# Gated product before the last bank, moved queue steps and ScalarE copies in long units of a gated attention and feed-forward kernel

## Chip, core and metric

The kernel runs on one core of a Trainium2 chip. The metric is the device time in microseconds of one execution. The engines are TensorE (PE), VectorE (DVE), ScalarE (ACT), GpSimd (POOL) and SyncE (SP), which issues all the transfers.

## The reference

The input is 2048 tokens of 576 features. Two branches are mixed by a gate per token.

```python
g = sigmoid((x * gate_w).sum(-1))
# a: 32 heads of 18, four segments of 512 tokens
for s in range(4):
    p = softmax(q_s @ k_s.T * scale + mask)  # keys later than the query are masked
    a_dot = p @ v_s
    a_mem = (phi(q_s) @ M) / (phi(q_s) @ z + 1e-6)
    o_s = sigmoid(beta) * a_mem + (1 - sigmoid(beta)) * a_dot
    M += phi(k_s).T @ v_s;  z += phi(k_s).sum()
a = concat(o_s) @ wo
# b: hidden size 4608
b = (silu(x @ w_gate) * (x @ w_up)) @ w_down
out = g * a + (1 - g) * b
```

Here phi(t) is t + 1 for positive t and exp(t) otherwise.

## The kernel before

Numbers are kept as pairs: a 16-bit high half and a low half that holds the rounding rest, so that a product is three matmuls. A high half is made by a copy, mostly on ScalarE, and its low half by a subtraction on VectorE or GpSimd.

The first stage runs over the four segments. For each of nine chains `n` (pairs `(m, u)` of a weight tile and q or k) `qk` makes 14 matmuls and casts the result; `mid` is a list of other small work that is put in between. For segments 1 to 3 the generator `upd_gen` adds the memory matrix of the segment before: it transposes phi of the keys and copies it to `kt` (512 columns on ScalarE, L514, and 64 on VectorE, L517). Eight value steps `v_step` and memory reads `mem_step` follow. `RSTEP` places the splits of the last 64 rows of x for the first token half in segment 2: `rest_split(j)` makes one of seven pieces, `rest_sum(j)` one of the sums that some pieces need. `FSUM` and `FSPLIT` place the same for the other rows in segment 3; `first_split(6, ...)` stands behind the first two value steps.

The second stage is the feed-forward part, in two token halves of 1024. Each half has 36 units `f`, one for each 128 hidden columns. A unit computes gate and up products of two token blocks by a scheme of seven products instead of eight, `seven(bank, j)`, j = 0 to 6, seven matmuls each. Block 0's gated row is `sg0`, block 1's `sg1`; `p5` is the up part of block 1. `sg1` needs products 4 and 5, but not product 6; `sg0` needs product 6. `split_by` makes their halves `hh` and `hl` by deferred steps.

Behind each product stands `tick()`, eight steps a unit (0 to 7); step 6 stands right behind step 5, and product 6 between steps 6 and 7. A step first runs what `defer(k, fn)` put off for it: k = 1 is the next step. Then it runs down groups and attention steps. A unit with `q = f % 3 == 0` and f > 0 is a long unit: it carries the 16 down groups of the three units before it (`feed`: eight 128-token tiles `i`, two column halves `hf`), nine matmuls each into one of two banks. Tiles 0 to 3 belong to block 0, tiles 4 to 7 to block 1. `down_end` (L1171, or L1169 for the first three units) adds the bank to `ya` on VectorE and so frees the bank. The groups begin in step 2: 2, 2, 3, 3, 3 and 3 in steps 2 to 7. Behind the last unit of the first half ten steps without products run the remaining 16 groups (`BREAK`).

Attention of all segments runs as a generator, `att_gen`, one bank of a head pair a step `tau`. In a long unit it advances 12 times. In an ordinary pair of heads ScalarE makes the exponential `pe` (L1006), GpSimd clears its upper triangle, then `p1` is its fp16 copy (L1102 on VectorE, L1104 on ScalarE) and `p2` the rest, on GpSimd (L1106). In the second half every second pair is "turned": the maximum is taken first, the exponential is L943, and `c_bank` copies it to fp16 on VectorE (L947) and takes the rest on GpSimd (L948). `later[0]` is true in the second half from unit 1 on.

Down weights are split by `d_split(f)`: ScalarE copy L1139 in the same step, VectorE low half L1140 one step later, a scaled third L1142 or L1144 after that, then a store `dc` for the second half. `rest_second` makes the rest pieces of the second half's tokens in steps behind unit 35. ScalarE's functions Exp and Silu need different tables; `exp_table()` runs a dummy Exp so that the load comes at a chosen place, and `gates()` makes the token gates with Exp.

Each engine runs its instructions in the order in which this program emits them. Units are told below by half and number; "unit 9" is the tenth of the first half.

Of the kernel before, what the change touches and what calls it, by code (L numbers as in the profile page):

```python
# [69 lines left out]
def gated_mix(ctx, tc, xT, xrest, wf, wfr, wfh, wd, wv, wo, beta, cmask, ident, bmask, out):  # L70
# [323 lines left out]
    with ExitStack() as st:  # L394
# [101 lines left out]
        def upd_gen(s):  # L496
            acc = [pair_tile([P, 3, MW]), pair_tile([P, 2, MW])]
            Mo, Mn = Mm[s % 2], Mm[(s + 1) % 2]
            for i in range(5):
# [8 lines left out]
                if i < 4:  # L508
# [8 lines left out]
                    nc.vector.tensor_copy(kt[:, 512:576], tb[:, 64:128])  # L517
# [143 lines left out]
        RSTEP = {2: (0, 3), 3: (5, -1), 4: (1, -4), 5: (4, -2), 6: (2,), 7: (-6,), 8: (6,)}  # L661
# [59 lines left out]
        def scan_load(t):  # L721
# [3 lines left out]
            if t in (21, 30):  # L725
# [3 lines left out]
        FSUM = {3: [(1, 0), (4, 0)], 4: [(2, 0), (1, 1)], 6: [(4, 1), (2, 1)], 7: [(6, 0)], 8: [(6, 1)]}  # L729
        FSPLIT = {2: [(0, 0)], 3: [(5, 0), (0, 1)], 4: [(1, 0), (4, 0)], 5: [(5, 1), (2, 0)], 6: [(1, 1), (3, 0)],  # L730
                  7: [(3, 1), (4, 1)], 8: [(2, 1)]}
        for s in range(NSEG):
            upd = upd_gen(s - 1) if s else None
            casts = []
            for n, (m, u) in enumerate(chains):
# [41 lines left out]
                qk(s, m, u, mid)  # L777
                flush(2)
# [19 lines left out]
            for n in range(8):  # L798
# [44 lines left out]
    with ExitStack() as st:  # L843
# [207 lines left out]
        def att_gen():  # L1051
            N = 10 * NB
            for tau in range(N + TL + VL + 5):
# [236 lines left out]
        later = [False]  # L1290
        turn_of = [()]
# [33 lines left out]
        def feed(half, f):  # L1325
            return [(f // CH, i, hf, hs, ds, half) for i in range(8) for hf in range(2)]
# [43 lines left out]
        def rest_second(rest):  # L1370
# [19 lines left out]
            def low(j):  # L1390
# [3 lines left out]
            todo = [(-1, load, 0), (0, high, 0), (0, high, 3), (1, low, 0), (1, low, 3), (4, load, 1), (11, high, 5),  # L1394
                    (11, total, 1), (12, low, 5), (12, high, 1), (13, total, 4), (13, low, 1), (14, total, 2),
                    (14, high, 4), (15, low, 4), (15, total, 6), (16, high, 2), (16, low, 2), (17, high, 6), (18, low, 6)]
# [37 lines left out]
        for pos, (half, f) in enumerate(seq):  # L1434
# [49 lines left out]
            def tick():  # L1484
# [5 lines left out]
                if half == 0:  # L1490
# [19 lines left out]
            later[0] = half == 1 and f > 0  # L1510
            turn_of[0] = () if pos < 24 else (1, 3)
# [154 lines left out]
```

## Time and profile before

| | |
|---|---|
| three runs | 1718.13, 1721.46, 1721.53 us |
| median | 1721.46 us |
| profiled execution, its own time | 1718.78 us |
| its span | 1717.1 us |
| busy: TensorE, VectorE, ScalarE, GpSimd | 98%, 79%, 63%, 52% |
| granted TensorE clock, mean | 0.998 |

The profile is of one execution. Rows of the order in time give start, duration, engine, line, operation, written and read tiles, shape and count; square brackets give how long the engine was idle before and what ended it. Line numbers are those of the kernel before.

### The profile page before, as it was taken

Reading aid. Unit: us, or ns where it says so; the run is one execution under the profiler, and the core shown is the slowest. Engines: PE = TensorE matmul, PEld = TensorE weight load, DVE = VectorE, ACT = ScalarE, POOL = GpSimd, SP = SyncE. Lnnn points to the kernel's source line nnn. Section 1 sums busy time; section 2 is a strip of 40 time slices with the busy share of each in tenths; the row PEclk is TensorE's granted clock in tenths of the full one; section 3 lists DMA queues with packets and bytes.
Section 4 is the critical chain, followed back from the end, with each engine's and each line's share of the span. In section 5 each row is a group of like instructions: output and inputs, shape, how many; then the busy total and the mean of one; then the engine's idle time right before and its main releaser. Section 6 shows DMA issues by size and latency. Waiting matters only on the chain.

```text
span 1717.1 us, 35318 instructions
## 1 busy us (share of the span) xinstructions
PE 1679.5 (98%) x12269; PEld 1077.8 (63%) x12269; DVE 1353.8 (79%) x3295; ACT 1076.6 (63%) x1930; POOL 889.2 (52%) x1191
## 2 busy tenths in 40 slices
PE   9999999999999999999999999999999999999999
PEld 7898865556655665565555656556656656655577
DVE  6687676789888988898886878788878788776466
ACT  7666567777777777767774654665556566565411
POOL 3336562266667665665452665465546565554121
PEclk9999999999999999999999999999999999999999
DMA  8666675666776675446535486796696597574544
GB/s 282 218 232 222 214 260 208 208 200 177 231 223 208 168 244 192 154 121 195 169 123 164 114 192 158 163 219 136 147 215 166 121 221 167 140 163 125 156 157 145
DMA packets 349542, 314.25 MB, mean 183 GB/s; under 512 B 201268, under 2 KB 266548, under 8 KB 349364
## 3 DMA queue, kind: packets, MB, share of 16 engines
q1 hardware_dynamic: 349364, 312.00, 63.5%
q8 instruction: 96, 1.57, 0.4%
q14 instruction: 82, 0.67, 0.1%
HBM read 186.15 MB, written 99.55 MB: 166 GB/s over the span
## 4 chain that ended last, share of the span: by engine, by line
PE 73%; DVE 12%; ACT 7%; issue 3%; DMA 3%; POOL 1%; SPq 1%; DVEq 0%; ACTq 0%; POOLq 0%
PE bank L1426 31%; PE bank L1162 18%; PE bank L223 8%; PE bank L1429 5%; PE bank L889 3%; PE bank L1002 2%; DVE ya L1171 1%; PE bank L1030 1%; ACT L1540 1%; DVE junk L907 1%; PE bank L1032 1%; PE bank L964 1%; DVE p L1102 1%; ACT row L1540 1%; DMA rc<-rt 1%
## 5 line engine op out<-in xcount | busy, mean ns | idle before, releaser
L1162 PE MATMUL bank<-dw,hh 128*128 128x320 f16 (+1 forms) x2304 | 437.5, 286 | 13.3 <-DVE ya L1171 8.9
L1162 PE MATMUL bank<-dw,hl 128*128 128x320 f16 (+1 forms) x1152 | 330.1, 287 | 3.8 <-DVE hl L1298 3.2
L1106 POOL TENSOR_TENSOR p<-pe,p 128x512 f16<-128x512 f32 x220 | 271.9, 1236 | 75.3 <-DVE p L1102 50.6
L1162 PEld LDWEIGHTS <-hh 128*128 128x128 f16 x2304 | 225.3, 98 | 99.9 <-issue 18.1
L1006 ACT ACTIVATE pe<-bank 128x512 f32<-128x512 f32 x220 | 130.1, 592 | 183.6 <-PE bank L1002 167.5
L1171 DVE SCALAR_TENSOR_TENSOR ya<-bank,sc,ya 128x320 f32<-128x320 f32 x352 | 176.2, 511 | 55.0 <-PE bank L1162 53.3
L1429 PE MATMUL bank<-xr,rh 128*128 128x512 f16 x504 | 191.0, 379 | 0.0
L907 DVE CUSTOM_DVE_ANT_0 junk<-bank,cm 128x128 bf16<-128x128 f32 (+2 forms) x352 | 169.3, 481 | 13.7 <-PE bank L889 7.3
L1298 DVE SCALAR_TENSOR_TENSOR hl<-hh,row 128x512 f16<-128x512 f16 x144 | 129.7, 902 | 45.7 <-ACT hh L1295 44.8
L1014 POOL TENSOR_SCALAR_AFFINE_SELECT pe<-pe 128x256 f32<-128x256 f32 (+1 forms) x220 | 89.3, 406 | 144.9 <-ACT pe L1006 137.3
L1162 PEld LDWEIGHTS <-hl 128*128 128x128 f16 x1152 | 112.7, 98 | 34.3 <-DVE hl L1298 3.8
L889 PE MATMUL bank<-kst,qst 108*128 108x512 bf16 (+3 forms) x512 | 124.5, 299 | 3.6 <-ACT pe L1006 2.9
L1002 PE MATMUL bank<-qst,kst 111*128 111x512 bf16 (+3 forms) x352 | 103.2, 300 | 1.1 <-DVE acc L975 1.1
L1102 DVE CAST p<-pe 128x512 f16<-128x512 f32 x203 | 103.3, 510 | 0.0
L369 POOL TENSOR_TENSOR ws<-raw 128x256 f32<-128x256 f32 x72 | 65.6, 912 | 63.4 <-DMA raw<-in_wf_dram 32.2
L1538 DVE TENSOR_TENSOR row<-bank,row 128x512 f32<-128x512 f32 x72 | 49.6, 689 | 60.9 <-ACT bank L1537 60.8
L223 PE MATMUL bank<-xo,qhi 128*128 128x512 f32 x288 | 92.5, 401 | 1.3 <-ACT xo L132 0.7
L466 POOL TENSOR_TENSOR q<-qr,q 128x512 bf16<-128x512 f32 x36 | 47.8, 1329 | 84.8 <-ACT q L465 77.0
L1295 ACT ACTIVATE hh<-row 128x512 f16<-128x512 f32 x144 | 89.0, 618 | 3.7 <-DVE row L1548 3.0
L1533 ACT ACTIVATE row<-bank 128x512 f32<-128x512 f32 x72 | 42.9, 596 | 73.7 <-PE bank L1429 73.7
L1537 ACT ACTIVATE bank<-bank 128x512 f32<-128x512 f32 x72 | 41.9, 581 | 72.8 <-PE bank L1429 70.9
L1429 PEld LDWEIGHTS <-rh 128*128 128x128 f16 x504 | 49.3, 98 | 59.6 <-issue 0.2
(1102 smaller groups left out, 4213.9 us busy)
## 6 DMA issues: line engine op xcount, KB each, us to landing
xo<-in_wf_dram SPq DMA_DIRECT2D x65, 320.0 KB
raw<-in_wf_dram SPq DMA_DIRECT2D x72, 256.0 KB
dc<-dw SPq DMA_DIRECT2D x36, 432.0 KB
dw<-dc SPq DMA_DIRECT2D x36, 432.0 KB
rh<-rc SPq DMA_DIRECT2D x72, 168.0 KB
draw<-in_wd_dram SPq DMA_DIRECT2D x36, 288.0 KB
xo<-in_xT_dram SPq DMA_DIRECT2D x33, 256.0 KB
vd<-vps SPq DMA_DIRECT2D x8, 912.0 KB
```

The costliest lines, as they stand in the source:

```text
L223: nc.tensor.matmul(t, st[n], mv[n], start=(n == 0), stop=(n == 13))
L889: nc.tensor.matmul(t[:, c:c + w], qs[:KR, pr, P * i:P * i + P], ks[:KR, pr, 0:w], start=True, stop=True)
L907: nc.vector.tensor_tensor_reduce(junk.bitcast(BF)[:, :w], t[:, c:c + w], cm[:, L - w:L], 1.0, -3.0e38, OP.add, OP.max, m[:, k:k + 1])
L1002: nc.tensor.matmul(t[:, c:c + w], ks[:KR + 3, pr, P * j:P * j + P], qs[:KR + 3, pr, P * j:L], start=True, stop=True)
L1006: nc.scalar.activation(pe, t, AF.Exp, scale=SCALE)
L1102: nc.vector.tensor_copy(p1, pe)
L1106: nc.gpsimd.tensor_sub(p2, pe, p1)
L1162: nc.tensor.matmul(t, p, d[:, q, cs], start=(f == CH * c and n == 0), stop=(f == CH * c + CH - 1 and n == 2))
L1171: nc.vector.scalar_tensor_tensor(ya[:, i, cs], t, inv[c], ya[:, i, cs], op0=OP.mult, op1=OP.add)
L1298: nc.vector.scalar_tensor_tensor(lo, hi, -STEP, src, op0=OP.mult, op1=OP.add)
L1426: nc.tensor.matmul(t, w[:, p, z], x[z][:, q], start=first and n == 0, stop=False, skip_group_check=True)
L1429: nc.tensor.matmul(t, rem[:, RPOS[j]], XR[j], start=False, stop=True, skip_group_check=True)
```

## The change

It has these parts.

- The 64-column copy to `kt` is made by ScalarE.
- Segment 2: the sum for rest piece 6 moves from chain 7 to chain 6, and its split from within chain 8 to behind it.
- Segment 3: the sum and split of pieces (6, 1) and (2, 1) move from chain 8 to behind the first value step; both splits of piece 6 follow one value step later.
- The dummy Exp: gone in unit 0 of the first half; in unit 3 the one behind product 0 is gone, and the gates are made behind both Silu rows.
- `sg1`'s product (L1549) comes before product 6: ahead of step 6 in units with q = 0 (all but the very first unit), behind step 6 in the others. Block 1's halves are made first, and the down groups start with tiles 4 to 7.
- Unit 35: the down weights' split is issued in step 2 instead of 5. The rest pieces of the second half from the tenth entry on come two steps later.
- A flag `calm`, true in the long units of the second half: there ScalarE makes `p1` and `c_bank`'s copy.

```diff
-                    nc.vector.tensor_copy(kt[:, 512:576], tb[:, 64:128])
+                    nc.scalar.activation(kt[:, 512:576], tb[:, 64:128], AF.Copy)
...
-        RSTEP = {2: (0, 3), 3: (5, -1), 4: (1, -4), 5: (4, -2), 6: (2,), 7: (-6,), 8: (6,)}
+        RSTEP = {2: (0, 3), 3: (5, -1), 4: (1, -4), 5: (4, -2), 6: (2, -6)}
...
-        FSUM = {3: [(1, 0), (4, 0)], 4: [(2, 0), (1, 1)], 6: [(4, 1), (2, 1)], 7: [(6, 0)], 8: [(6, 1)]}
+        FSUM = {3: [(1, 0), (4, 0)], 4: [(2, 0), (1, 1)], 6: [(4, 1), (2, 1)], 7: [(6, 0)]}
-                  7: [(3, 1), (4, 1)], 8: [(2, 1)]}
+                  7: [(3, 1), (4, 1)]}
...
                 qk(s, m, u, mid)
+                if (s, n) == (2, 8):
+                    rest_split(6)
...
-                    if n < 2:
-                        first_split(6, n)
+                    if n == 0:
+                        first_split(2, 1)
+                        first_sum(6, 1)
+                    if 1 <= n < 3:
+                        first_split(6, n - 1)
...
-            nc.vector.tensor_copy(pq[:, 0:L], lg)
+            if calm[0]:
+                nc.scalar.activation(pq[:, 0:L], lg, AF.Copy)
+            else:
+                nc.vector.tensor_copy(pq[:, 0:L], lg)
...
-                    if later[0] or z % 5 not in turn_of[0]:
+                    if not calm[0] and (later[0] or z % 5 not in turn_of[0]):
...
-            return [(f // CH, i, hf, hs, ds, half) for i in range(8) for hf in range(2)]
+            return [(f // CH, i, hf, hs, ds, half) for i in (4, 5, 6, 7, 0, 1, 2, 3) for hf in range(2)]
...
-            todo = [..., (4, load, 1), (11, high, 5), (11, total, 1), (12, low, 5), ..., (17, high, 6), (18, low, 6)]
+            todo = [..., (4, load, 1), (13, high, 5), (13, total, 1), (14, low, 5), ..., (19, high, 6), (20, low, 6)]
...
-                    if f == 2 and k > 4 or f > 2 and (q, k) in ((1, 1), (1, 7), (2, 5 + int(f < FT - 1))):
-                        g = k - 5 if f == 2 else f - 1 if k == 1 else f
+                    if f == 2 and k > 4 or f > 2 and (q, k) in ((1, 1), (1, 7), (2, 6 if f < FT - 1 else 2)):
+                        g = k - 5 if f == 2 else f - 1 if (q, k) == (1, 1) else f
...
+            calm[0] = half == 1 and q == 0 and f > 0
...
-            if half == 0 and q == 0 and f:
+            if half == 0 and q == 0 and f > CH:
                 exp_table()
-                if f == CH:
-                    gates()
...
             nc.scalar.activation(sg1, y, AF.Silu, scale=iw[f // 4])
-            if (half or q == 0) and not cps:
+            if (half or q == 0 and f) and not cps:
                 exp_table()
+                if half == 0 and f == CH:
+                    gates()
             tick()
+            if q == 0 and pos:
+                nc.vector.scalar_tensor_tensor(sg1, p5, hk[f // 4], sg1, op0=OP.mult, op1=OP.mult)
             tick()
+            if q or not pos:
+                nc.vector.scalar_tensor_tensor(sg1, p5, hk[f // 4], sg1, op0=OP.mult, op1=OP.mult)
             seven(xx, 6, False)
             nc.vector.scalar_tensor_tensor(sg0, xx, hk[f // 4], sg0, op0=OP.mult, op1=OP.mult)
-            nc.vector.scalar_tensor_tensor(sg1, p5, hk[f // 4], sg1, op0=OP.mult, op1=OP.mult)
-            split_by(2, hh[:, 0], hl[:, 0], sg0, int(q < CH - 1))
-            split_by(3, hh[:, 1], hl[:, 1], sg1)
+            split_by(2, hh[:, 1], hl[:, 1], sg1, int(q < CH - 1))
+            split_by(3, hh[:, 0], hl[:, 0], sg0)
             tick()
```

More of the change, by code (lines that the diff above doesn't have):

```diff
@@ L1290, in gated_mix @@
         later = [False]
+        calm = [False]
         turn_of = [()]
@@ L1392, in low @@
                 nc.vector.scalar_tensor_tensor(t, source(j)[32:64], sx[32:64], t, op0=OP.mult, op1=OP.subtract)
-            todo = [(-1, load, 0), (0, high, 0), (0, high, 3), (1, low, 0), (1, low, 3), (4, load, 1), (11, high, 5),
-                    (11, total, 1), (12, low, 5), (12, high, 1), (13, total, 4), (13, low, 1), (14, total, 2),
-                    (14, high, 4), (15, low, 4), (15, total, 6), (16, high, 2), (16, low, 2), (17, high, 6), (18, low, 6)]
+            todo = [(-1, load, 0), (0, high, 0), (0, high, 3), (1, low, 0), (1, low, 3), (4, load, 1), (13, high, 5),
+                    (13, total, 1), (14, low, 5), (14, high, 1), (15, total, 4), (15, low, 1), (16, total, 2),
+                    (16, high, 4), (17, low, 4), (17, total, 6), (18, high, 2), (18, low, 2), (19, high, 6), (20, low, 6)]
             return [(o, lambda fn=fn, j=j: fn(j)) for o, fn, j in todo]
```

## The prediction

> **What bounds the kernel now.** The profile's first part comes first: who is busy.
>
> ```profile
> PE 1679.5 (98%) x12269; PEld 1077.8 (63%) x12269; DVE 1353.8 (79%) x3295; ACT 1076.6 (63%) x1930; POOL 889.2 (52%) x1191
> ```
>
> TensorE is busy 1679.5 of 1717.1 us, so 37.6 us is the most that removing waits can give, apart from stretches where its clock is halved. No matmul is added or removed; the question is which waits go and which come. Hence the view of waits with TensorE as the waiting engine, first for 300 to 900 us (first half), then 940 to 1620 us (second half); columns: total, times, longest.
>
> ```profile
> PE bank L1162 <- DVE ya L1171: 4.8, 8, 1.0
> PE bank L889 <- ACT pe L1006: 2.3, 6, 0.4
> ```
>
> ```profile
> PE bank L1162 <- DVE ya L1171: 4.1, 10, 0.9
> PE bank L889 <- ACT pe L1006: 0.6, 2, 0.3
> ```
>
> In both halves the main wait is for VectorE's accumulation `ya`, which frees a bank of the down product; in the long units VectorE paces the end. Then the busy time by stretches, for the granted clock (the column after POOL) around the two worst places.
>
> ```profile
> 270.00:276.00 6.00, 3.99 (x20) 1.67 (x18) 3.22 (x6) 5.97 (x12) 0.00 (x0) 1.00 0.88 279
> 276.00:282.00 6.00, 5.41 (x26) 3.04 (x26) 3.54 (x10) 2.83 (x8) 1.45 (x2) 0.72 1.01 383
> 901.00:904.00 3.00, 0.54 (x3) 0.21 (x4) 3.00 (x4) 2.35 (x5) 2.00 (x2) 1.00 0.00 0
> 904.00:910.00 6.00, 6.00 (x36) 4.22 (x36) 3.40 (x7) 0.46 (x1) 0.32 (x1) 0.72 0.98 317
> ```
>
> Behind each idle cluster (2.0 of 6 us and 2.5 of 3 us) the mean clock of the next six microseconds falls to 0.72: 0.28 times 6, so 1.7 us of work is lost in each spell, by this estimate.
>
> The Trainium skill, "TensorE: Matmul & The Clock Gate", Part 1, names an idle window of about 3.4 us as what halves the clock, and asks for no idle gap above that. The rows show halving after clusters without so long a gap, so the measurement decides; by the Trainium skill's gap rule no spell would be there to save and the gain below would be 3.4 us smaller.
>
> **The change, part by part.**
>
> *The kt cast to ScalarE* (12 times, segments 1 to 3). Two waits go:
>
> ```profile
> 65.76 0.35 PE L505 MATMUL bank<-vf,kt 128*64 128x76 f32 x2 [1.06 <-DVE kt L517]
> 196.41 0.35 PE L505 MATMUL bank<-vf,kt 128*64 128x76 f32 x2 [0.72 <-DVE kt L517]
> ```
>
> The cast queues on ScalarE right behind the 512-column cast that the same group of matmuls needs anyway, so it is there before its use. ScalarE gets 12 short casts; what stands behind each is the next chain's copy, with three banks in rotation as cover; without it each would cost its own length. Bounds 0 and -1.8; I take -1.8.
>
> *Segment 2: the rest piece 6 moves.* Its subtraction goes to GpSimd one chain earlier, its split behind chain 8.
>
> ```profile
> 158.30 0.74 DVE L249 SCALAR_TENSOR_TENSOR xr<-xo,sc,xr 32x512 f16<-32x512 f32 x1
> 159.07 0.69 DVE L468 SCALAR_TENSOR_TENSOR ph<-bank,ph 128x512 f32<-128x512 f32 x1
> 159.82 0.93 PE L550 MATMUL bank<-Mm,ph 128*128 128x152 f32 x6 [1.35 <-DVE ph L468]
> ```
>
> `ph` no longer stands behind 0.74 us of split. -0.74 is one bound, -1.35 the other, if the earlier subtraction also unblocks VectorE; I take -1.2. Late next is the first value step's own chain.
>
> *Segment 3: pieces (6,1) and (2,1) move behind the first value step.*
>
> ```profile
> 219.96 0.46 DVE L486 TENSOR_TENSOR r<-bank,vps 128x288 f32<-128x288 f32 x1 [0.21 <-ACT vps L485]
> 220.47 1.85 PE L223 MATMUL bank<-vw,xo 128*128 128x288 f32 x12 [0.83 <-DVE r L486]
> ```
>
> VectorE itself waited 0.21 for ScalarE here, so taking a split off VectorE does not bring L486 forward. Bounds -0.83 and +0.75 (one split more, later); I take 0.
>
> *Fewer table loads.* Without the dummy exponential in units 0 and at the head of 3, two Exp loads and the two Silu loads that followed them go.
>
> ```profile
> 245.88 1.28 ACT L1419 ACT_TABLE_LOAD   x1
> 248.53 1.46 PE L1426 MATMUL bank<-xo,wo__2849 128*128 128x512 f16 x6 [0.53 <-ACT bank L1519]
> ```
>
> The load stands ahead of the bank copy that TensorE waits for: -0.5. In unit 3:
>
> ```profile
> 271.50 1.28 ACT L1419 ACT_TABLE_LOAD   x1
> 275.57 0.74 DVE L377 SCALAR_TENSOR_TENSOR wo__3111<-ws,sc,wo__3111 128x512 f16<-128x512 f32 x1
> 275.70 0.30 PE L1162 MATMUL bank<-dw,hh 128*128 128x320 f16 x1 [1.14 <-DVE dw L1140]
> 276.59 0.30 PE L1162 MATMUL bank<-dw,hl 128*128 128x320 f16 x1 [0.59 <-DVE dw L1142]
> 276.72 0.38 PE L1162 MATMUL bank<-dw,hh 128*128 128x256 f16 x2
> ```
>
> ScalarE's `hh`, and behind it VectorE's `hl`, `dw` and the scaled third, come at least 1.28 us earlier. The 1.14 goes; the third still has L377's 0.74 ahead of it, so I leave 0.5 of the second wait: -1.2. With so little idle time left the half-clock spell goes: -1.7. Bounds 0 and -3.4.
>
> *Last unit of the first half.* The down weights' split is issued three steps earlier, the other columns' rest pieces two steps later (five ScalarE copies, five VectorE low halves, four GpSimd subtractions), and the product that needs no last bank is made first and used first.
>
> ```profile
> 900.59 1.36 DVE L1549 SCALAR_TENSOR_TENSOR row<-row,sc 128x512 f32<-128x512 f32 x1
> 901.39 0.45 PE L1162 MATMUL bank<-dw,hh 128*128 128x320 f16 x2 [0.89 <-ACT hh L1295]
> 901.88 1.37 DVE L1142 TENSOR_SCALAR dw<-dw 128x576 f16<-128x576 f16 x1
> 903.90 0.31 PE L1162 MATMUL bank<-dw,hl 128*128 128x320 f16 x1 [2.06 <-DVE hl L1298]
> ```
>
> Of the 2.95 us, the 1.37 leaves the path, and one product of 1.36 runs under the last bank's matmuls: -2.7, and the second spell -1.7. Bounds 0 and -4.7. The rest pieces, two steps later, end inside the next unit, behind its first three products, each issued ahead of its own bank's use; one piece late would cost up to a low half of this shape, 0.74 (L249 above). I take 0. One `dc` store moves forward with the split on the DMA queue; it lands in memory that is read only in the second half.
>
> *The last unit of all*, the same order:
>
> ```profile
> 1632.87 2.42 DVE L1298 SCALAR_TENSOR_TENSOR hl<-hh,row 128x512 f16<-128x512 f16 x2
> 1634.70 0.31 PE L1162 MATMUL bank<-dw,hl 128*128 128x320 f16 x1 [1.10 <-DVE hl L1298]
> ```
>
> The wait ends inside the 2.42 us of the two low halves; no row tells how much of that is their own work and how much is blocking, so an earlier start may not be wholly an earlier end. Bounds 0 and -1.1; -0.5.
>
> *Long units of both halves: the product moved ahead of step 6.* This one costs. In unit 9:
>
> ```profile
> 408.50 0.75 DVE L377 SCALAR_TENSOR_TENSOR wo__4684<-ws,sc,wo__4684 128x512 f16<-128x512 f32 x1
> 409.16 0.55 DVE L1171 SCALAR_TENSOR_TENSOR ya<-bank,sc,ya 128x320 f32<-128x320 f32 x1
> 409.76 0.43 PE L1162 MATMUL bank<-dw,hh 128*128 128x320 f16 x2
> 414.02 0.78 DVE L1549 SCALAR_TENSOR_TENSOR row<-row,sc 128x512 f32<-128x512 f32 x1
> ```
>
> The product now at 414.02 goes in ahead of L377 at 408.50. `ya` ends at 409.71 and the matmul that needs its bank starts at 409.76: no slack. An operation of this kind holds the queue 0.66 (408.50 to 409.16) to 0.78 us, so TensorE waits some 0.7 us more. At the old place it held up nothing: that step shows no wait. Eleven long units of the first half: +7.7. Bounds 0 and +15 (1.36 each, from 900.59). In the short units the product now waits for ScalarE's Silu instead of the last bank; only the other product stands behind it, which waits for that bank anyway: 0.
>
> *Second half, long units: some 130 casts from VectorE to ScalarE* (12 attention steps a unit, one cast each). The busy time of their two lines in the eleven units, then one cast on ScalarE, and from the order in time two rows of unit 15:
>
> ```profile
> sum 388.00, DVE 36.16; mean DVE 3.29
> sum 388.00, DVE 30.76; mean DVE 2.80
> L1104 ACT ACTIVATE p<-pe 128x512 f16<-128x512 f32 x17 | 10.6, 622 | 0.0
> 1242.84 1.28 DVE L1549 SCALAR_TENSOR_TENSOR row<-row,sc 128x512 f32<-128x512 f32 x1
> 1244.57 0.38 PE L1162 MATMUL bank<-dw,hh 128*128 128x256 f16 x2 [0.87 <-DVE ya L1171]
> ```
>
> VectorE gets back 6.1 us in each long unit, more than the 0.7 that the moved product puts before step 6; behind bank 6 the product is gone as well, which is the wait at 1244.57. Up to the whole 4.1 goes. ScalarE takes some 12 times 0.62, 7.3 us a unit. Its own busy time in these units and in the first half's eleven:
>
> ```profile
> sum 388.00, PE 380.19 PEld 258.96 DVE 307.97 ACT 191.75 POOL 204.71; mean PE 34.56 PEld 23.54 DVE 28.00 ACT 17.43 POOL 18.61
> sum 396.70, PE 384.50 PEld 257.94 DVE 339.34 ACT 273.45 POOL 234.38; mean PE 34.95 PEld 23.45 DVE 30.85 ACT 24.86 POOL 21.31
> ```
>
> 17.4 becomes 24.7, as much as the first half bears with its 2.3 us of waits for `pe`, 1.7 more than the second half has now. The casts read what was ready two steps before, so I take a third of that, +0.6, and -4.1 for VectorE: -3.5. Queued behind the casts are the exponentials of the next step and, through `p1`, GpSimd's low halves. Bounds -4.1 and +14 (below).
>
> *Groups in the order 4 to 7, 0 to 3*: as many matmuls, only a match to the order of `hh`: 0.
>
> **The sum.** The idle column starts at a matmul's modelled end: the one at 276.59 lasts 0.30, but the next starts 0.13 later. Each wait removed gives 0.17 more than it shows; some twelve go: -2.0. -1.8 -1.2 -0.5 -2.9 -4.4 -0.5 +7.7 -3.5 -2.0 = -9.1 us. The profiled execution took 1718.78 us (span 1717.1), so 1709.7. It lies at the lower end of the three runs (median 1721.46, lowest 1718.13); I add 1.3, half of that distance: **1711**.
>
> **The rivals.**
> *The moved product is free in the first half.* If VectorE had time in hand before step 6, 7.7 us fall away: 1703. For it: VectorE is 30.85 busy of 36 us. Against it: unit 9's `ya` without slack.
> *The moved product costs 1.3.* It has two inputs in SBUF, and 900.59 and 1242.84 show it at 1.36 and 1.28, against 0.78 at 414.02. At 1.3 in all eleven, 6.6 us more: 1717.6, no change to be measured. The Trainium skill, "SBUF — State Buffer", "SBUF: two separate sides", says that a VectorE operation with two SBUF inputs and a GpSimd operation that reads SBUF block each other for a whole instruction; the spread of the three durations fits it, but the row of a long unit is the short one.
> *The change does not do what it says at units 3 and 35.* Waits remain, and the clock still halves: both spells (3.4) and two thirds of the 3.9 us of waits come back, 6.0: 1717. Against it: both clusters hang on instructions that really move.
> *Slower: ScalarE becomes the bound in the second half's long units.* It has two table loads, 1.28 us each, in step 5, and one cast more for each of 12 steps. If at two steps of each unit a cast of 0.62 lies ahead of an exponential that TensorE waits for, 11 times 1.24 is +13.6, and the 3.5 is not gained: 1728. It decides once more than 9 us of this reach TensorE. Against it: the first half bears the same load.
>
> **How the numbers follow.** Forecast 0.50 (its own range 1704 to 1716); free product 0.20; dear product 0.10; units 3 and 35 unchanged 0.07; ScalarE bound 0.13. Range 1701 to 1722: it leaves out the slower case and the far end of the free one. A measurement of this kernel can tell 0.2%, 3.4 us: faster 0.70, same 0.17, slower 0.13.
>
> **What would show it.** four table loads fewer; no wait for `kt`; the clock at 1.00 behind both places; the wait for `ya` L1171 up from 4.8 to some 12 us in the first half and below 1 in the second; waits for `pe` up slightly. If the first half's `ya` waits stay at 4.8, or the second half's `pe` waits pass 5 us, the prediction is wrong there.

## The result and the profile after

| | before | after |
|---|---|---|
| median | 1719.80 us | 1735.16 us |
| lowest to highest | 1717.06 to 1721.53 | 1734.84 to 1736.13 |
| profiled execution, its span | 1717.1 | 1733.1 |

The ratio is 1.0092, with a 95% interval from 1.0074 to 1.0109: 15.4 us slower, where 9 us faster was forecast. Both medians are over four runs, those of before with one more than were shown. The first part of the page after the change:

```profile
PE 1682.2 (97%) x12269; PEld 1077.7 (62%) x12269; DVE 1315.2 (76%) x3155; ACT 1139.6 (66%) x2064; POOL 878.2 (51%) x1191
```

VectorE is busy 38.6 us less than before and ScalarE 63.0 more, as planned, and yet the kernel is slower. So the loss isn't in a sum of work; it is in where the work stands. The waits of TensorE show where, first for 300 to 900 us (first half), then for 940 to 1640 us (second half). Columns: total, times, longest.

```profile
PE bank L1170 <- DVE ya L1179: 19.7, 13, 2.4
PE bank L894 <- ACT pe L1014: 2.4, 6, 0.4
```

```profile
PE bank L1170 <- DVE ya L1179: 3.7, 5, 1.4
PE bank L894 <- ACT pe L1014: 2.4, 5, 1.0
```

L1170, L1179, L894 and L1014 are L1162, L1171, L889 and L1006 of before. In the first half the wait for `ya` rose from 4.8 to 19.7 us, by 14.9; the span grew by 16.0. (The two aren't parts of one sum. From first matmul to first matmul the ten long units 6 to 33 of the first half grew by 19.7 us in all, and the rest of the kernel got 3.7 shorter.) It isn't more waits so much as longer ones: 2.4 us at the longest, where 1.0 was. In the second half it hardly fell (4.1 to 3.7), and the wait for exponentials rose (0.6 to 2.4). The order in time of unit 9 shows one of the long waits whole; first VectorE, then GpSimd, then TensorE:

```profile
409.13 0.75 DVE L1557 SCALAR_TENSOR_TENSOR row<-row,sc 128x512 f32<-128x512 f32 x1
409.79 1.65 DVE L377 SCALAR_TENSOR_TENSOR wo__4682<-ws,sc,wo__4682 128x512 f16<-128x512 f32 x1
411.36 0.54 DVE L1179 SCALAR_TENSOR_TENSOR ya<-bank,sc,ya 128x320 f32<-128x320 f32 x1
```

```profile
409.36 1.52 POOL L1114 TENSOR_TENSOR p<-pe,p 128x512 f16<-128x512 f32 x1 [1.34 <-PE bank L1010]
```

```profile
411.95 0.43 PE L1170 MATMUL bank<-dw,hh 128*128 128x320 f16 x2 [1.60 <-DVE ya L1179]
```

The product stands ahead of L377 as forecast and holds the queue 0.66 us. But L377, 0.75 us long at this place before, now takes 1.65. The row of GpSimd in unit 9 of the kernel before:

```profile
408.73 1.53 POOL L1106 TENSOR_TENSOR p<-pe,p 128x512 f16<-128x512 f32 x1 [1.34 <-PE bank L1002]
```

There L377, begun at 408.50, was 0.23 us ahead of this subtraction (L1114 after); now the product begins ahead of the subtraction, and L377 comes while the subtraction is under way. 0.66 and 0.90 make 1.56, and TensorE waits 1.60. Some of the waits are followed by a lower clock. Two stretches of the busy time, in units 27 and 30, each with a wait of 1.96 us (the column behind POOL is the granted clock):

```profile
760.00:780.00 20.00, 17.76 (x143) 11.35 (x142) 16.34 (x44) 7.44 (x13) 13.94 (x21) 0.91 0.26 78
820.00:840.00 20.00, 17.54 (x146) 11.66 (x144) 16.74 (x45) 7.60 (x13) 13.88 (x20) 0.91 0.29 82
```

0.09 of 20 us are 1.8 us of work lost in each, by this estimate; these two units grew by 2.8 and 3.1 us, the other long ones of the first half from 6 on by 1.2 to 2.0. The length of a wait alone doesn't decide it: behind the longest one, 2.39 us in unit 6, the clock stays at 1.00.

### The profile page after: what moved, and what is told of

The parts are those of the page before. It is cut to its first block, busy times and chain, and to the rows that moved or that the text cites. A ratio compares the mean times of both kernels' runs of the same rounds, so it can differ in the third digit from the quotient of the medians.

```text
span 1733.1 us, 35354 instructions
## 1 busy us (share of the span) xinstructions
PE 1682.2 (97%) x12269; PEld 1077.7 (62%) x12269; DVE 1315.2 (76%) x3155; ACT 1139.6 (66%) x2064; POOL 878.2 (51%) x1191
## 3 DMA queue, kind: packets, MB, share of 16 engines
q8 instruction: 96, 1.57, 0.4%
## 4 chain that ended last, share of the span: by engine, by line
PE 75%; DVE 9%; ACT 9%; issue 3%; DMA 2%; POOL 1%; SPq 1%; DVEq 0%; ACTq 0%; POOLq 0%
PE bank L1435 30%; PE bank L1170 19%; PE bank L223 10%; PE bank L1438 5%; PE bank L894 3%; PE bank L1010 2%; ACT L1548 1%; PE bank L1038 1%; ACT L1428 1%; ACT row L1548 1%; DVE ya L1179 1%; DVE junk L912 1%; ACT pe L1014 1%; PE bank L505 1%; PE bank L972 1%
## 5 line engine op out<-in xcount | busy, mean ns | idle before, releaser
L1170 PE MATMUL bank<-dw,hh 128*128 128x320 f16 (+1 forms) x2304 | 436.5, 286 | 27.0 <-DVE ya L1179 23.4
L1170 PE MATMUL bank<-dw,hl 128*128 128x320 f16 (+1 forms) x1152 | 330.0, 286 | 0.9 <-DVE dw L1150 0.6
L1114 POOL TENSOR_TENSOR p<-pe,p 128x512 f16<-128x512 f32 x220 | 271.1, 1233 | 65.0 <-DVE p L1110 35.2
L1170 PEld LDWEIGHTS <-hh 128*128 128x128 f16 x2304 | 225.2, 98 | 112.8 <-issue 32.6
L1014 ACT ACTIVATE pe<-bank 128x512 f32<-128x512 f32 x220 | 130.2, 592 | 181.0 <-PE bank L1010 169.8
L1179 DVE SCALAR_TENSOR_TENSOR ya<-bank,sc,ya 128x320 f32<-128x320 f32 x352 | 178.1, 512 | 82.5 <-PE bank L1170 80.7
L1170 PEld LDWEIGHTS <-hl 128*128 128x128 f16 x1152 | 112.5, 98 | 31.9 <-DVE hl L1307 2.9
L894 PE MATMUL bank<-kst,qst 108*128 108x512 bf16 (+3 forms) x512 | 125.0, 299 | 5.5 <-ACT pe L1014 4.8
L1529 ACT ACTIVATE bank<-bank 128x512 f32<-128x512 f32 x72 | 41.9, 582 | 69.5 <-PE bank L1438 59.1
L1545 ACT ACTIVATE bank<-bank 128x512 f32<-128x512 f32 x72 | 41.9, 581 | 65.3 <-PE bank L1438 63.4
```

Of the source, the lines that this page charges most:

```text
L894: nc.tensor.matmul(t[:, c:c + w], qs[:KR, pr, P * i:P * i + P], ks[:KR, pr, 0:w], start=True, stop=True)
L1014: nc.scalar.activation(pe, t, AF.Exp, scale=SCALE)
L1114: nc.gpsimd.tensor_sub(p2, pe, p1)
L1170: nc.tensor.matmul(t, p, d[:, q, cs], start=(f == CH * c and n == 0), stop=(f == CH * c + CH - 1 and n == 2))
L1179: nc.vector.scalar_tensor_tensor(ya[:, i, cs], t, inv[c], ya[:, i, cs], op0=OP.mult, op1=OP.add)
```

## The experiments

In the expectations unit 0.9 is unit 9 of the first half and 1.9 that of the second. A ratio is to the kernel before, measured on the same chip in the same experiment, and a difference to the kernel before is between these two medians. Kernels of different experiments are best compared by their ratios.

**Where the loss is: the product, in the first half.** The changed kernel, with the product ahead in the second half alone:

```diff
-            if q == 0 and pos:
+            if q == 0 and half:
...
-            if q or not pos:
+            if q or not half:
```

> The changed kernel, but in the long units of the first half sg1's product is made behind step 6 again; ahead of it only in the second half. Theory A (the product ahead of step 6 displaces VectorE's other work there, above all the weight split of L377, into GpSimd's subtraction of L1114, and costs 1.5 to 2.1 us in each of the ten long units 6 to 33 and more where the clock falls): the 19.7 us by which these units grew go, and the time is 1735 - 20 = 1715 (1711 to 1719). Theory B (the moved product is nearly free, and the loss of the first half comes with other parts, the new order of groups or the moved splits): 1731 to 1736. Theory C (the moved product costs its 0.66 to 0.7 us of queue and no more, the rest comes with other parts): 1735 - 11 x 0.7 = 1727.

Measured: 1720.9 us, ratio 1.0013 [1.0004, 1.0023], by the two ratios (1.0092 to 1.0013) some 14 us less than the changed kernel. Theory A; but 5.9 us more than it said, so something else costs too. The other way round, this part alone in the kernel before:

```diff
             tick()
+            ahead = half == 0 and q == 0 and f > 0
+            if ahead:
+                nc.vector.scalar_tensor_tensor(sg1, p5, hk[f // 4], sg1, op0=OP.mult, op1=OP.mult)
             tick()
...
-            nc.vector.scalar_tensor_tensor(sg1, p5, hk[f // 4], sg1, op0=OP.mult, op1=OP.mult)
+            if not ahead:
+                nc.vector.scalar_tensor_tensor(sg1, p5, hk[f // 4], sg1, op0=OP.mult, op1=OP.mult)
```

> The kernel before with one edit: sg1's product ahead of step 6 in the long units of the first half. Theory A (product ahead costs 1.5 to 2.1 us in each long unit): 1720 + 11 x 1.8 = 1740 (1736 to 1744). Theory B (product nearly free): 1719 to 1722. Theory C (0.7 us each): 1727.

Measured: 1736.7 us, ratio 1.0110 [1.0096, 1.0124], +17.8 us from one instruction moved in eleven units. Its waits from 300 to 900 us are those of the changed kernel:

```profile
PE bank L1162 <- DVE ya L1171: 19.6, 13, 2.4
```

**Why: the product, L377 or GpSimd.** The same kernel, with the product behind L377 instead of ahead of it (put at the end of the deferred work of step 6):

```diff
-                nc.vector.scalar_tensor_tensor(sg1, p5, hk[f // 4], sg1, op0=OP.mult, op1=OP.mult)
+                defer(1, lambda f=f, p5=p5, sg1=sg1: nc.vector.scalar_tensor_tensor(
+                    sg1, p5, hk[f // 4], sg1, op0=OP.mult, op1=OP.mult))
```

> The kernel before with sg1's product ahead of step 6 in the long units of the first half, but issued behind the weight split of L377 there, not ahead of it. Theory K (VectorE's operations with both operands in SBUF and GpSimd's subtraction L1114 don't run beside each other; whichever of VectorE's two comes second waits for the subtraction): the product itself now takes 1.6 us, and the time is that of the product ahead of L377, 1736.7 (1734 to 1739). Theory L (it is L377 alone that suffers, by its place): 1719 + 11 x 0.7 = 1727 or less.

Measured: 1736.9 us, ratio 1.0100 [1.0084, 1.0115]. Groups of instructions from 300 to 900 us, the moved product (written and read tiles, shape, count, busy time, mean ns), first with it ahead of L377, then behind:

```profile
L1548 DVE SCALAR_TENSOR_TENSOR row<-row,sc 128x512 f32<-128x512 f32 x10 | 7.5, 746 | 0.0
```

```profile
L1548 DVE SCALAR_TENSOR_TENSOR row<-row,sc 128x512 f32<-128x512 f32 x10 | 16.4, 1645 | 0.0
```

And unit 9 with it behind, in the order in time of VectorE and GpSimd:

```profile
412.67 0.75 DVE L377 SCALAR_TENSOR_TENSOR wo__4684<-ws,sc,wo__4684 128x512 f16<-128x512 f32 x1
413.34 1.65 DVE L1548 SCALAR_TENSOR_TENSOR row<-row,sc 128x512 f32<-128x512 f32 x1
```

```profile
410.04 1.16 POOL L1106 TENSOR_TENSOR p<-pe,p 128x512 f16<-128x512 f32 x1
...
412.91 1.53 POOL L1106 TENSOR_TENSOR p<-pe,p 128x512 f16<-128x512 f32 x1 [1.34 <-PE bank L1002]
```

All ten products went from 0.75 to 1.65 us, and L377 back to 0.75. It's the second place that is dear, whoever stands there. GpSimd is the partner, if the loss goes when its subtraction is cut; the pair of kernels for that, without and with the product ahead, covers 64 of its 512 columns in the first half and leaves the rest of `p2` at zero:

```diff
-                    nc.gpsimd.tensor_sub(p2, pe, p1)
...
+                    w2 = L if later[0] else 64
+                    nc.gpsimd.tensor_sub(p2[:, 0:w2], pe[:, 0:w2], p1[:, 0:w2])
```

> The kernel before, in which GpSimd's subtraction of L1106 covers 64 of 512 columns in the first half (the rest of p2 stays zero, so this part of the attention's low half is left out; everything else is done). By itself a base for the next run. Theory K (VectorE's two-operand reads and this subtraction exclude each other): the stretched weight splits of the long units fall from 1.64 to 0.75 us, and the time falls a little, 1714 to 1719. If GpSimd is no part of it: 1718 to 1720.

> The same cut in the kernel with sg1's product ahead of step 6 in the long units of the first half (the low half of the attention's probabilities is left out in the same columns). Against the run without the product ahead, theory K: what is left is the product's own place in the queue, at most 0.7 us in each of eleven units and less where the queue had room, so +2 to +8 us where it was +17.8 with the whole subtraction. Theory M (the queue alone, or the ScalarE, or TensorE's own order makes the loss, and GpSimd's subtraction only happens to lie there): +14 to +18 again.

Measured: 1716.8 us without, ratio 0.9993 [0.9984, 1.0003], and 1722.4 with, 1.0022 [1.0012, 1.0031]. The product ahead costs 5.6 us where it cost 17.8. L377 in unit 9 of the second, and the waits of 300 to 900 us, without and with the product ahead:

```profile
408.34 0.75 DVE L1555 SCALAR_TENSOR_TENSOR row<-row,sc 128x512 f32<-128x512 f32 x1
409.00 0.80 DVE L377 SCALAR_TENSOR_TENSOR wo__4689<-ws,sc,wo__4689 128x512 f16<-128x512 f32 x1
```

```profile
PE bank L1169 <- DVE ya L1178: 3.4, 5, 1.2
```

```profile
PE bank L1169 <- DVE ya L1178: 10.5, 14, 1.9
```

What is left, 7.1 us of waits and 5.6 us of time, is put down to the product's place in the queue: 0.5 us a unit, less than the 0.7 forecast. Two thirds of the loss, 12.2 of 17.8 us, go with the subtraction, and theory M falls.

**The rest of the loss: the order.** Without the product ahead anywhere and without the copies, the changed kernel keeps the moves and the new order:

```diff
-            if q == 0 and pos:
-                nc.vector.scalar_tensor_tensor(sg1, p5, hk[f // 4], sg1, op0=OP.mult, op1=OP.mult)
...
-            if q or not pos:
+            if True:
                 nc.vector.scalar_tensor_tensor(sg1, p5, hk[f // 4], sg1, op0=OP.mult, op1=OP.mult)
...
-            calm[0] = half == 1 and q == 0 and f > 0
```

> The changed kernel with the product behind step 6 in every unit and the copies on VectorE: what is left are the moves in the queues, the new order of groups, one table load less at three places and kt on ScalarE. By the prediction's own terms these are worth -1.8 -1.2 -0.5 -1.2 -1.7 -2.7 -1.7 -0.5 -2.0 = -13.3: 1720 - 13 = 1707. By the unit lengths of the two profiles (-2.3 in stage one, +0.9 in unit 0.0, -0.5, -0.6, -4.1, -1.2): 1720 - 8 = 1712, which theory A expects, with no growth left in the long units of the first half. If the group order or the moved pieces cost in the long units (theory B): 1725 or more.

Measured: 1718.2 us, ratio 0.9998 [0.9989, 1.0007]. The 13.3 us of the prediction are not there, nor the 8 of the unit lengths. Then the order alone, in the kernel before:

```diff
+            nc.vector.scalar_tensor_tensor(sg1, p5, hk[f // 4], sg1, op0=OP.mult, op1=OP.mult)
             seven(xx, 6, False)
...
-            split_by(2, hh[:, 0], hl[:, 0], sg0, int(q < CH - 1))
-            split_by(3, hh[:, 1], hl[:, 1], sg1)
+            split_by(2, hh[:, 1], hl[:, 1], sg1, int(q < CH - 1))
+            split_by(3, hh[:, 0], hl[:, 0], sg0)
```

(with the groups from tile 4 on and the product's old line gone)

> The kernel before with the new order alone: sg1's product (still behind step 6), its split first, sg0 after it, and the groups from block 4 on. Theory I: 1719 + 5.5 = 1724.5. Theory J and the prediction, which costed the order at nothing: 1718 to 1720.

Measured: 1722.6 us, ratio 1.0022 [1.0013, 1.0032], +3.4. The order isn't free. Unit 12 of it, VectorE and GpSimd behind product 6:

```profile
472.94 1.64 DVE L1547 SCALAR_TENSOR_TENSOR row<-row,sc 128x512 f32<-128x512 f32 x1
474.50 0.74 DVE L1549 SCALAR_TENSOR_TENSOR row<-bank,sc,row 128x512 f32<-128x512 f32 x1
475.16 0.47 DVE L1171 SCALAR_TENSOR_TENSOR ya<-bank,sc,ya 128x256 f32<-128x256 f32 x1
```

```profile
472.70 1.32 POOL L1106 TENSOR_TENSOR p<-pe,p 128x512 f16<-128x512 f32 x1
```

and the same unit before:

```profile
470.30 0.74 DVE L1548 SCALAR_TENSOR_TENSOR row<-bank,sc,row 128x512 f32<-128x512 f32 x1
470.96 0.98 DVE L1549 SCALAR_TENSOR_TENSOR row<-row,sc 128x512 f32<-128x512 f32 x1
471.87 0.47 DVE L1171 SCALAR_TENSOR_TENSOR ya<-bank,sc,ya 128x256 f32<-128x256 f32 x1
```

```profile
470.07 1.33 POOL L1106 TENSOR_TENSOR p<-pe,p 128x512 f16<-128x512 f32 x1
```

The subtraction begins 0.23 to 0.24 us ahead of the pair of products in both. Before, `sg0`'s product stood first; it reads a bank, takes 0.74 beside the subtraction, and the other comes when most of that is over. In the new order the product with both inputs in SBUF stands first and waits the subtraction out: from the first product to `ya` 2.22 us instead of 1.57. It's the same mechanism at a second place, but only a part of the loss. Matmul by matmul, unit 12 falls behind by 0.66 us: 0.35 at the bank that this `ya` frees, 0.17 at a low half `hl` (L1298) and 0.14 at the bank that ScalarE's L1519 copies. And the short units 4 to 34 of the first half grew by 2.1 us, every third one by some 0.2. Unit 11 shows what happens there, with no subtraction of GpSimd beside the products; VectorE, then ScalarE:

```profile
430.99 0.75 DVE L1547 SCALAR_TENSOR_TENSOR row<-row,sc 128x512 f32<-128x512 f32 x1 [1.22 <-ACT row L1542]
431.65 0.74 DVE L1549 SCALAR_TENSOR_TENSOR row<-bank,sc,row 128x512 f32<-128x512 f32 x1
```

```profile
432.49 0.58 ACT L1519 ACTIVATE bank<-bank 128x512 f32<-128x512 f32 x1 [0.26 <-DVE row L1549]
```

`sg0`'s product, which reads the last bank, now stands behind `sg1`'s, which waits for ScalarE's second Silu (L1542). ScalarE's copy goes into that bank and waits for `sg0`'s product. Counted from the unit's start, TensorE's third product, which waits for this copy, starts 0.07 us later than before, and its fifth, which waits for VectorE's addition L1530, 0.20. How the 3.4 us divide between these places is not tried.

**The copies.** The changed kernel without them, with the product ahead:

```diff
-            calm[0] = half == 1 and q == 0 and f > 0
```

> The changed kernel, but the fp16 copies in the long units of the second half are made by VectorE as before. Theory D (ScalarE's copies relieve VectorE by what the prediction said, and something else took it back): the second half's long units grow by 0.3 to 0.4 us each, 1735 + 4 = 1739. Theory E (the copies on ScalarE cost in exp's place what they save on VectorE): 1734 to 1736. Theory F (the copies on ScalarE cost more than they save, the product ahead saves): 1729 to 1733.

Measured: 1740.2 us, ratio 1.0129 [1.0115, 1.0143]. Theory D: beside a product that stands ahead they are worth some 6 us by the two ratios (1.0129 to 1.0092), 5.0 by the two medians, and 4.0 by the lengths of the second half's eleven long units in the two profiles.

With them, with the product behind:

```diff
-            if q == 0 and pos:
-                nc.vector.scalar_tensor_tensor(sg1, p5, hk[f // 4], sg1, op0=OP.mult, op1=OP.mult)
...
-            if q or not pos:
+            if True:
```

> The changed kernel with the product behind step 6 in every unit; the copies on ScalarE and the new order of sg1 before sg0 and of the groups stay. The runs so far: without copies and with the product behind, 1718.2; without copies and with it ahead, 1740.2; with copies and with it ahead in the second half alone, 1720.9. Theory G (copies and product are independent in the second half: copies save about 5, the product ahead costs about 5 there too): 1718 - 5 = 1713 (1711 to 1716). Theory H (the copies save only what the product ahead costs, since both stand at the same place): 1717 to 1721.

Measured: 1717.5 us, ratio 0.9992 [0.9983, 1.0001]. Theory H: beside a product that stands behind they are worth 0.7 by the medians (1718.2 without) and 1.0 by the ratios, no difference that can be told.

This one with the order of before:

```diff
-            return [(f // CH, i, hf, hs, ds, half) for i in (4, 5, 6, 7, 0, 1, 2, 3) for hf in range(2)]
+            return [(f // CH, i, hf, hs, ds, half) for i in range(8) for hf in range(2)]
...
-            nc.vector.scalar_tensor_tensor(sg1, p5, hk[f // 4], sg1, op0=OP.mult, op1=OP.mult)
             seven(xx, 6, False)
             nc.vector.scalar_tensor_tensor(sg0, xx, hk[f // 4], sg0, op0=OP.mult, op1=OP.mult)
+            nc.vector.scalar_tensor_tensor(sg1, p5, hk[f // 4], sg1, op0=OP.mult, op1=OP.mult)
-            split_by(2, hh[:, 1], hl[:, 1], sg1, int(q < CH - 1))
-            split_by(3, hh[:, 0], hl[:, 0], sg0)
+            split_by(2, hh[:, 0], hl[:, 0], sg0, int(q < CH - 1))
+            split_by(3, hh[:, 1], hl[:, 1], sg1)
```

> As the run before, and also the order as it was: sg0's product and split first, the groups from block 0 on. What is left of the change are kt on ScalarE, the table loads, the moved pieces, the drain, and the copies in the second half. Theory I (the new order of splits and groups costs 0.3 to 0.4 us in each long unit of the first half and 0.2 in each third unit, 3.4 + 2.1 = 5.5 us, and saves nothing in the second half): 1713 - 5.5 = 1707.5 (1705 to 1711). Theory J (that loss belongs to the moved pieces of segments 2 and 3 or to the time that stage one ends earlier, and stays): 1712 to 1715.

Measured: 1712.5 us, ratio 0.9959 [0.9946, 0.9971]: 5.0 less than in the new order, theory I in size; its 1707.5 was built on theory G's 1713.

And the copies alone, in the kernel before:

```diff
-            nc.vector.tensor_copy(pq[:, 0:L], lg)
+            if calm[0]:
+                nc.scalar.activation(pq[:, 0:L], lg, AF.Copy)
+            else:
+                nc.vector.tensor_copy(pq[:, 0:L], lg)
...
-                    if later[0] or z % 5 not in turn_of[0]:
+                    if not calm[0] and (later[0] or z % 5 not in turn_of[0]):
...
+            calm[0] = half == 1 and q == 0 and f > 0
```

> The kernel before with the copies alone: in the long units of the second half ScalarE makes the fp16 copies. The prediction: -3.5 us, 1715.5. By the waits of the runs so far (the waits for ya in the second half fall from 4.1 to 2.2 us, those for exp rise from 0.6 to 2.4): no change, 1718 to 1720.

Measured: 1717.8 us, ratio 0.9995 [0.9987, 1.0003], -0.8, which can't be told from no change. The waits of 940 to 1640 us of this kernel:

```profile
PE bank L1165 <- DVE ya L1174: 2.2, 5, 0.8
PE bank L889 <- ACT pe L1009: 2.1, 4, 1.0
```

The prediction gave the copies 4.1 us of VectorE's waits against 0.6 of ScalarE's; they take 1.9 and give back 1.5. Last, the kernel of the product alone, with it ahead in the other half:

```diff
-            ahead = half == 0 and q == 0 and f > 0
+            ahead = half == 1 and q == 0
```

> The kernel before with sg1's product ahead of step 6 in the long units of the second half alone. The prediction took it for hidden once the copies are gone from VectorE, and here they are not. Theory Q (the product ahead costs some 0.4 us in each of these units while VectorE still makes the copies, and the copies on ScalarE make room for it and for nothing else): +4 to +5, 1723. Theory R (its cost of 3 to 5 in the runs so far came with the new order): 1718 to 1720.

Measured: 1719.9 us, ratio 1.0014 [1.0005, 1.0023], +2.0. By its range this is theory R, at the upper end. But the ratio is clear of 1 and the order here is the old one, so the product costs something in the second half too, though less than theory Q said; the waits for `ya` (940 to 1640 us) rise from 4.1 to

```profile
PE bank L1162 <- DVE ya L1171: 6.8, 8, 1.7
```

**The moved pieces.** All of them, which is the kernel of the old order without the copies:

```diff
-            calm[0] = half == 1 and q == 0 and f > 0
```

> The kernel before with kt on ScalarE, the moved pieces, the table loads and the last unit's split alone: no copies, no product ahead, the order of splits and groups as before. The prediction's terms for these: -1.8 -1.2 -0.5 -1.2 -1.7 -2.7 -1.7 -0.5 -2.0 = -13.3, 1706. By the unit lengths of the runs so far (stage one -2.5, unit 0.0 +0.9, units 0.1 to 0.5 -1, unit 0.35 -4.1, the rest 0): 1719 - 6.5 = 1712.5; with the copies, 1712.5 was measured.

Measured: 1711.5 us, ratio 0.9966 [0.9954, 0.9979], -7.0, about what the unit lengths said. Two of the pieces alone in the kernel before, kt and then unit 35:

```diff
-                    nc.vector.tensor_copy(kt[:, 512:576], tb[:, 64:128])
+                    nc.scalar.activation(kt[:, 512:576], tb[:, 64:128], AF.Copy)
```

> The kernel before with the move of kt to ScalarE alone. The prediction: -1.8, 1717. If unit 0.0, whose inputs come no earlier, takes back what stage one gains (theory P): -0.5 to -1, within what can be told from no change, 1718.

Measured: 1715.2 us, ratio 0.9984 [0.9975, 0.9992], -2.7.

```diff
-            todo = [..., (11, high, 5), ..., (18, low, 6)]
+            todo = [..., (13, high, 5), ..., (20, low, 6)]
...
-                    ... (q, k) in ((1, 1), (1, 7), (2, 5 + int(f < FT - 1))):
-                        g = k - 5 if f == 2 else f - 1 if k == 1 else f
+                    ... (q, k) in ((1, 1), (1, 7), (2, 6 if f < FT - 1 else 2)):
+                        g = k - 5 if f == 2 else f - 1 if (q, k) == (1, 1) else f
```

> The kernel before with the moves of unit 0.35 alone: its down weights are split four steps earlier and the rest pieces of the second half two steps later. The prediction: -2.7 -1.7 = -4.4, 1714.2. By the length of unit 0.35 in the run of all the pieces, -3.15: 1715.5.

The split is issued in step 2 instead of 5, so three steps earlier, not four. Measured: 1714.7 us, ratio 0.9980 [0.9972, 0.9989], -3.2. The waits of 0.89 and 2.06 us in unit 35 have become one of 1.37. Behind this idle cluster, now 1.5 of 3 us, the clock stays at 1.00:

```profile
899.00:902.00 3.00, 1.52 (x11) 0.81 (x10) 2.96 (x3) 2.25 (x4) 2.66 (x2) 1.00 1.04 317
905.00:911.00 6.00, 6.00 (x52) 4.83 (x50) 3.74 (x7) 0.00 (x0) 1.18 (x1) 1.00 0.45 165
```

This alone doesn't show that the move keeps the clock up. In the kernel with the product ahead in the second half, which leaves unit 35 as it was, 2.55 of 3 us are idle at this place (2.46 in the profile of before), and yet the clock stays at 1.00:

```profile
901.00:904.00 3.00, 0.45 (x3) 0.12 (x3) 3.00 (x4) 2.41 (x5) 2.10 (x2) 1.00 0.00 0
904.00:910.00 6.00, 6.00 (x49) 4.74 (x50) 4.61 (x9) 0.97 (x2) 1.65 (x2) 1.00 0.89 293
```

So the spell comes in some executions and not in others. Over whole executions the mean clock was 1.000 in 6 of 29 of the kernel before and in 7 of 11 of this one. Between these alone the medians are 1716.3 and 1714.6: 1.7 us apart, near the 1.6 that the waits of unit 35 lost. The rest of the 3.2 is put down to rarer spells; no run separates the two.

In unit 3 a new wait took the gain, in the profile of all the pieces. ScalarE, VectorE and TensorE's waits from 262 to 302 us:

```profile
281.31 0.74 ACT L140 ACTIVATE xo<-xo 128x640 f32<-128x640 f32 x1 [1.93 <-DMA xo<-in_wf_dram]
282.05 0.58 ACT L1544 ACTIVATE bank<-bank 128x512 f32<-128x512 f32 x1
```

```profile
282.65 0.69 DVE L1545 TENSOR_TENSOR row<-bank,row 128x512 f32<-128x512 f32 x1 [2.76 <-ACT bank L1544]
283.26 0.54 DVE L1177 TENSOR_SCALAR ya<-bank,sc 128x320 f32<-128x320 f32 x1
```

```profile
PE bank L1170 <- DVE ya L1177: 3.6, 2, 2.5
```

ScalarE stands at a square of weights whose transfer isn't there yet; behind it stand an eviction, VectorE's addition and TensorE. One edit takes this square out of the way:

```diff
-                    ((2, 2, 3, 4, 5, 6, 6, 7)[k], lambda: square(box[0], 20 + 9 * i + k))]
+                    ((2, 2, 3 + int(i == 2), 4, 5, 6, 6, 7)[k], lambda: square(box[0], 20 + 9 * i + k))]
```

> The run of the pieces alone, and in unit 0.3 one square (L140, the third of four) one step later. In that run's unit 0.3 ScalarE stood 1.93 us at this square for its transfer, with the eviction L1544 queued behind it, and TensorE waited 2.7 us for ya behind that. Theory N (the table loads' time in unit 0.3 was saved and lost again in this wait for a transfer): the wait of 2.5 us goes, 1711.5 - 2.5 = 1709. Theory O (the unit's length is set by its transfers as a whole, and the wait comes back at a later square or at a weight): 1711 to 1712.

Measured: 1711.3 us, ratio 0.9968 [0.9957, 0.9979]: no change, theory O. The wait for `ya` is down to 0.6, and another stands in its place (265 to 305 us):

```profile
PE bank L894 <- DMA kst<-stk: 2.8, 2, 2.5
...
PE bank L1170 <- DVE ya L1177: 0.6, 1, 0.6
```

In the run of all the pieces the transfers take all of the 16 engines' time around the square (the last but one column), and behind the wait the clock falls here too. Around the other run's wait, last, their share is 0.68:

```profile
278.00:284.00 6.00, 3.45 (x25) 2.25 (x23) 2.44 (x6) 4.07 (x11) 0.00 (x0) 0.97 1.03 393
284.00:290.00 6.00, 6.00 (x33) 3.73 (x32) 3.36 (x13) 2.66 (x5) 0.64 (x1) 0.74 0.73 245
```

```profile
290.00:296.00 6.00, 2.80 (x20) 1.86 (x21) 3.45 (x12) 2.17 (x5) 1.45 (x2) 1.00 0.68 213
```

So the first wait stands in a stretch full of transfers; what held the transfer of the second is open.

**The account.** From the kernels with one part alone: pieces -7.0, copies -0.8, order +3.4, product in the first half +17.8, in the second +2.0. The sum is +15.4, and +15.4 was measured. Parts do act on each other: the copies (next to nothing to 6), and the order, which cost 3.4 alone and 5.0 beside the pieces and the copies. That the sum fits this well is partly luck. The pieces alone (1711.5) are faster than both kernels: 0.34% faster than before, and by the two ratios (0.9966 to 1.0092) 1.2% faster than the changed one; the copies add nothing to them (1712.5).

## Why the prediction was wrong

- **The moved product, +0.7 each and +7.7 in the first half, is the step that failed**, by its size: +1.6 of wait in unit 9, +17.8 us over eleven units, and +2.0 more in the second half, where it was taken for covered. The place (the queue ahead of `ya`, no slack) was right, and the sign named for it came: the waits for `ya` in the first half rose from 4.8 us, though to 19.7 and not to 12; those in the second half stayed at 3.7, where below 1 was named. The price was read from how long such an operation takes, not from what runs on GpSimd beside the operation that it pushes back.
- The rival of the dear product named the mechanism and drew a wrong conclusion: it looked for the stretch in the moved product, whose row of a long unit was short. In the result the product is indeed short (0.75) and the instruction behind it is long (1.65). The Trainium skill, "SBUF — State Buffer", "SBUF: two separate sides", says that whichever of the two starts first has the shared ports for its whole instruction; the runs agree (0.75 for the first, 1.65 for the second, in both orders), and by this rule the question was who would start when.
- **Order at 0 failed as well**: +3.4. One reason given was that in the short units only the other product stands behind the moved one. Behind that product stands ScalarE's copy into its bank, for which TensorE's next unit waits: +2.1 us in the short units of the first half. In the long ones the subtraction beside the pair adds to it.
- **Copies -3.5 failed**: -0.8 alone, not to be told from 0. VectorE's waits fell by 1.9 of 4.1, and ScalarE's rose by 1.5, not 0.6. The slower rival, ScalarE as the bound, named the right engine but not the cause of the loss: its waits stayed at 2.4, below the 5 that was set as a sign.
- kt, -1.8: right, -2.7 alone, and its wait is gone. The segments' -1.2 is not to be seen: the wait of 1.35 for `ph` is gone, but the waits for `r` L486, 0.83 before, are now (the changed kernel up to 245 us)

```profile
PE bank L223 <- DVE r L486: 2.1, 3, 0.8
```

- Unit 0, -0.5: it grew by 0.9 in every kernel with all the pieces. TensorE comes to it 2.3 us earlier in the changed kernel, and waits for inputs that come only 1.4 us earlier (L377 at 233.06 for 234.49):

```profile
233.89 1.04 PE L1435 MATMUL bank<-xo,wo__2633 128*128 128x512 f16 x4 [0.51 <-DVE wo__2633 L377]
235.82 1.46 PE L1435 MATMUL bank<-xo,wo__2633 128*128 128x512 f16 x6 [0.68 <-ACT bank L1529]
```

- Unit 3, -2.9: between +1.1 and -1.1 us in the kernels with all the pieces, and between +1.2 and -1.7 in those without, so nothing that can be told. The spell of -1.7 in this term is no fixed part of the kernel: of the kernels that leave unit 3 as it was, the profiles of before and of the copies alone have it, and those of kt, of unit 35 and of the product ahead in the second half don't.
- Unit 35, -4.4: -3.2 alone, without the earlier product, which was 1.36 of the term; with it unit 35 is 4.1 us shorter in the changed kernel. The clock is at 1.00 there as forecast, but with the unit as it was it is so in some runs too, so the -1.7 was right only for some executions. The last unit, -0.5: no wait is left behind 1640 us in the changed kernel, the 1.10 of before is gone, and from that unit's first matmul on it is 1.2 us shorter. The -2.0 for matmuls' ends had assumed that removed waits stay removed; it was not tried by itself.
- The range ended at 1722. The dear product alone gave 1717.6; without the copies' gain, with the order's loss and the second half's product it would have come to 1717.6 + 2.7 + 3.4 + 2.0 = 1725.7, and with the measured 17.8 for 14.3 to 1729. No case had these together, and the one slower rival was another mechanism.

## What to carry to other kernels

Before an instruction is put into a queue that has no slack, look at what the engine that works beside it does in the 1 to 2 us behind it, and at which operation is pushed into that: the cost may be the stretch of the one behind, not the length of the one moved. Here an operation that reads a bank stood beside GpSimd's work where one that reads two SBUF tiles couldn't, so the order of two equal products mattered. A spell of low clock in one profile is not a sure gain: other executions of the same kernel may not have it. Test parts one at a time: here a sound gain of 7 us lay under losses of 23.

## What the runs showed of the hardware

In all rows shown VectorE's operations with two SBUF inputs and GpSimd's subtraction of two SBUF tiles excluded each other, in both directions: the subtraction went from 1.16 to 1.53 us where VectorE's came first, and VectorE's from 0.75 to 1.65 where the subtraction did. A VectorE product with one input in a bank took 0.74 beside the same subtraction. Waits of 1.96 us were followed by a mean clock of 0.91 over 20 us, and one of 2.39 us in the same execution by none. An idle cluster of 2.5 of 3 us was followed by 0.72 over 6 us in one execution and by 1.00 in that of another kernel.
